# First quads with the mask added by TensorE in PSUM, first products one quad later, summary rows by DMA, and three native groups of w_out

## The chip, the cores and the metric

The kernel runs on one core of a Trainium2 chip. The core has TensorE (matrix products into PSUM), VectorE (shown as DVE), ScalarE (ACT), GpSimd (POOL), SyncE (SP, here the issuer of nearly all transfers) and 16 DMA engines between DRAM and the on-chip memory SBUF. The metric is the device time of one execution in microseconds; the median of several runs is compared. Each engine works through its own instructions in order and waits on semaphores for the others.

## The reference

Inputs: q, k, v of shape (4 batches, 8 heads, 768 positions, 64), and the two weight matrices w_in (512 x 2048) and w_out (2048 x 512), all float32.

```python
k_sum = k.reshape(B, H, nb, block, D).max(axis=3)      # block = 32, nb = 24
v_sum = v.reshape(B, H, nb, block, D).mean(axis=3)
scores_l = scale * np.matmul(q, k.transpose(0, 1, 3, 2))
mask_l = np.abs(pos[:, None] - pos[None, :]) < window  # window = 16
scores_s = scale * np.einsum('bhsd,bhnd->bhsn', q, k_sum) + np.log(block)
scores_all = np.concatenate([np.where(mask_l, scores_l, -1e9), scores_s], axis=-1)
a = softmax(scores_all)
x = matmul(a, concatenate([v, v_sum])) -> (3072 tokens, 512)
h = x @ w_in
sp = np.maximum(h, 0.0) + np.log1p(np.exp(-np.abs(h)))
g = h * erf(sp)
out = g @ w_out
```

So each query sees its neighbours within 15 positions and 24 summaries of the whole sequence; a two-layer network with the activation h · erf(softplus(h)) follows.

## The kernel before, in words

**Tiling.** The 3072 tokens are six chunks of 512. A *quad* is one chunk and one pair of heads: four quads to a chunk, 24 in all. For a quad, the queries are taken in eight blocks of 64; each block needs a window of 96 keys and the 24 summaries, 120 columns. `scores` (line 434 on) makes them on TensorE into two PSUM banks, `softmax` adds the mask (lines 471 and 475), takes the maximum (479), the exponential with a sum (484) and divides (488 to 496). `transp` turns the weights by TensorE (506), ScalarE copies them out (510), and `av` (531) multiplies by the values. `xsplit` splits the result into a high part xh and a low part xl (236 and 547).

A *period* k is one chunk and one of four column groups of the hidden layer: 24 periods. In a period, `mm1` (line 570) makes the four hidden tiles of the group by products in a reduced form of float32: high x high, low x high and high x low, three products for one. `hout`, `logs`, `erfs` (581, 594, 599) compute the activation, `gsplit` multiplies and splits it (606, or 611, 236 and 618), and `mm2` (631 or 635) adds its product with w_out into four banks.

**Two forms of the second product.** For the first chunk `mm2` uses the native float32 product with w_out unsplit (line 631, tile a32s); for all others the split form of three products (line 635). `gsplit` follows: no split of the activation in the first chunk (line 606).

**Weights.** They come in as pairs of 32-bit words and VectorE puts each together in three steps (284, 287, 290). w_in's are split at once by `split`: ScalarE makes the high part (236), VectorE the low part (306). w_out's are put together into slots named in `WHOLE`, and split later by `parts`: groups 2 and 3 in period 3, groups 0 and 1 in period 4. Large SBUF slots w0 to w13 are shared in time. Not all split weights fit, so numbers 4 to 7 are stored to DRAM (`put`) and loaded again for each chunk (`get`) into the slots named in `HOME`.

**The first chunk's quads.** Quads 0 to 3 take their keys straight from the natural layout (tiles kf, qf), their maxima from `ksum_first` (388). The value means come from `vsum_first`: six products with a selection matrix (394), a copy by ScalarE (397), and four copies by GpSimd (399) which spread the 24 mean rows over the eight blocks of each quad's value tile vwf. Their scores lie in the banks pa, h0 and h1, o0 and o1, then h0 and h1 again; the same banks take the first hidden tiles (`hbanks`). After scores and softmax of all four, a loop does transpose, weighted sum, split and the first products of each quad in turn.

**Order.** A planner (class `Plan`) holds all operations with an assumed duration on an engine. `due` sets due times backwards from TensorE's order; `order` then runs a list schedule over the assumed durations, with TensorE allowed to pick among the next operations of its order, and transfers as a serial queue on SP. What comes out is the fixed order of instructions on every engine. Ahead of the first operation on TensorE stand `WARM` fillers (line 673), products of zeros into an unused bank; until the bank o3 is first used, `busy` puts more of them where the plan leaves TensorE idle.

Of the kernel before, what the change touches and what calls it, by code (L numbers as in the profile page):

```python
# [36 lines left out]
WARM = 20  # L37
# [126 lines left out]
def block_attention_mlp(ctx: ExitStack, tc: tile.TileContext, q_t, k_nat, k_win, v_tok, v_nat, v_win, w_in, w_out, out):  # L164
# [67 lines left out]
    def dma(kb, fn, r=(), w=(), **kw):  # L232
        return P.add({"SP": max(0.45, kb / 330.0)}, lambda e: fn(), r, w, **kw)
# [10 lines left out]
    WHOLE = {0: 11, 1: 10, 2: 8, 3: 9}  # L244
    HOME = {0: 12, 1: 13, 2: 11, 3: 8, 4: 9, 5: 10, 6: 9, 7: 10}
# [25 lines left out]
    def convert(u):  # L271

        w, s, m = f"w{raw_slot(u)}", {}, number(u)
        home = f"gl{u[2]}" if u[0] == "i" else f"a{m}"

        def a():
            if u[0] == "i":
# [14 lines left out]
        on({"DVE": 0.69}, lambda e: a(), [w], [home] if u[0] == "i" or u[2] else frees(WHOLE[u[1]]))  # L292
        on({"DVE": 1.22}, lambda e: b(), [w, home], [home])
        on({"DVE": 1.22}, lambda e: c(), [w, home], [home])
        if u[0] == "i":
            split(u, raw_slot(u), home, lambda: s["t"])
# [87 lines left out]
    def load_vw_first(p):  # L384
        dma(393, lambda: nc.sync.dma_start(out=st[p]["vw"][0:LW], in_=v_win[0, p]), w=[f"vwf{p}"])
# [4 lines left out]
    def vsum_first(bank):  # L390
# [7 lines left out]
        for p in range(NP):  # L398
            on({"POOL": 1.3}, lambda e, p=p: e.tensor_copy(st[p]["vw"][LW:NK], vsum[LW:NK, p:p + 1, :].to_broadcast([NS, NB, 128])), [f"vsum0{p}"], [f"vwg{p}"])
# [20 lines left out]
    def load_quad_v(qd):  # L420
# [6 lines left out]
        dma(393, go, w=["vw"])  # L427
# [5 lines left out]
    def scores(qd, banks=("pa",)):  # L433
# [3 lines left out]
        def go():  # L437
# [3 lines left out]
            s["both"] = tiles["pa"] if banks == ("pa",) else None  # L441
            for i in range(NI):
                for c in range(2):
                    j = 2 * i + c
                    for a in range(2):
# [8 lines left out]
                        for n, rhs in parts:  # L454
                            n += i * NK
                            nc.tensor.matmul(sc[a][o, n:n + rhs.shape[-1]], lhsT=s["qb"][r, 64 * j:64 * j + 64], rhs=rhs, start=True, stop=True)  # L456
        if qd >= NP:
            pe(1.06, go, ["qb", "kw"], banks)
        else:
            pe(1.4, go, [f"qf{qd}", f"kf{qd}", f"ksum0{qd}"], banks)  # L460

    def softmax(qd, banks=("pa",)):
# [5 lines left out]
        def add(e):  # L468
            t = s["pr"] = sb([128, 2 * NI, NK], F32, "pr") if qd >= NP else prs[qd // 2][:, qd % 2]
            if s["both"] is not None:  # L470
                e.tensor_tensor(t.rearrange("q (a i) c -> q a i c", a=2), s["both"][:, :, 0:NI * NK].rearrange("q a (i c) -> q a i c", i=NI),  # L471
                                mk.unsqueeze(1).to_broadcast([128, 2, NI, NK]), op=ALU.add)
            else:
                for a in range(2):
                    e.tensor_tensor(t[:, NI * a:NI * a + NI], s["sc"][a][:, 0:NI * NK].rearrange("q (i c) -> q i c", i=NI), mk, op=ALU.add)
# [398 lines left out]
```

## Time and profile before

| | before |
|---|---|
| median of 3 runs, us | 654.64 (654.37 to 656.39) |
| the profiled execution's own time, us | 654.22 |
| its span, first to last instruction, us | 652.4 |
| mean granted TensorE clock | 0.997 |
| instructions | 10447 |
| TensorE products busy | 642.3 us, 98% |
| VectorE busy | 399.6 us, 61% |
| ScalarE busy | 429.5 us, 66% |
| GpSimd busy | 24.1 us, 4% |
| moved by DMA | 89.02 MB, mean 136 GB/s |

The profile is one execution recorded by the hardware. A line of a group names the line of the kernel, the engine, the operation, the tile written and the tile read, shapes and count; after the bar stand the busy time in all, the mean of one in nanoseconds, and the idle time of that engine just before, with what ended it. A float32 product is recorded as two records in the native form. The chain of waits is followed backwards from the last instruction, at each step to what released it. "issue" is time in which an engine waited for nothing that the profile shows.

### The profile page before, as it was taken

What the parts mean: (1) busy time and instruction counts of PE and PEld (TensorE: products, weight loads), DVE (VectorE), ACT (ScalarE), POOL (GpSimd) and SP (SyncE); (2) the same over time, 40 slices, a digit from 0 to 9 for tenths busy, and PEclk for the clock granted to TensorE, in tenths of its full rate; (3) what the DMA queues carried; (4) which work ended last, traced back from release to release, by engine and by line L of the source; (5) the groups of instructions that cost most, each with busy time, mean ns of one, the idle gap of its engine ahead of it and who ended that gap; (6) DMA issues with size and microseconds to landing.
All of it is one profiled execution on the core that took longest, in us unless ns stands there. A gap on an engine that the chain in (4) does not pass through costs nothing.

```text
span 652.4 us, 10447 instructions
## 1 busy us (share of the span) xinstructions
PE 642.3 (98%) x4216; PEld 497.7 (76%) x4224; DVE 399.6 (61%) x507; ACT 429.5 (66%) x770; POOL 24.1 (4%) x52
## 2 busy tenths in 40 slices
PE   9799999999999999999999999999999999999997
PEld 4477656657588888888888888888888888888886
DVE  4899999866666755656656556456457355334432
ACT  2476999787976675865854964945866754763570
POOL 3301000000000000000000000000000000000000
PEclk9899999999999999999999999999999999999999
DMA  8997654355373425464315442206352103140014
GB/s 323 286 333 264 225 142 158 130 205 206 108 272 90 126 62 168 159 227 109 102 37 194 132 151 66 78 1 206 85 186 77 31 0 115 65 144 1 1 51 143
DMA packets 27872, 89.02 MB, mean 136 GB/s; under 512 B 2992, under 2 KB 7856, under 8 KB 22704
## 3 DMA queue, kind: packets, MB, share of 16 engines
q1 hardware_dynamic: 27248, 87.83, 41.9%
q8 instruction: 33, 0.54, 0.3%
q10 hardware_dynamic: 576, 0.52, 0.2%
q14 instruction: 15, 0.12, 0.1%
HBM read 75.89 MB, written 10.49 MB: 132 GB/s over the span
## 4 chain that ended last, share of the span: by engine, by line
PE 97%; ACT 1%; issue 1%; DVE 0%
PE h L570 39%; PE ops L635 34%; PE ops L631 9%; PE px L531 4%; PE idle L673 3%; PE pa L456 3%; PE pa L506 3%; PE vs L394 1%; PE h L456 0%; ACT L832 0%; PE vt L352 0%; PE o L456 0%; ACT wt L581 0%; ACT wt L594 0%; ACT ptr L510 0%
## 5 line engine op out<-in xcount | busy, mean ns | idle before, releaser
L570 PE MATMUL h<-xh,w 128*128 128x512 f32 x768 | 250.9, 397 | 0.0
L635 PE MATMUL ops<-w,gh 128*128 128x512 f32 x640 | 202.1, 392 | 0.0
L570 PEld LDWEIGHTS h<-xh,w 128*128 128x128 f32 x768 | 144.2, 188 | 32.6 <-issue 1.5
L581 ACT ACTIVATE wt<-h 128x512 f32<-128x512 f32 x96 | 56.8, 596 | 144.9 <-DVE hc L236 79.3
L570 PE MATMUL h<-xl,w 128*128 128x512 f32 x384 | 149.6, 389 | 0.0
L635 PEld LDWEIGHTS ops<-w,gh 128*128 128x128 f32 x640 | 120.5, 188 | 25.2
L236 DVE COPY hc<-h 128x512 f32<-128x512 f32 x90 | 62.0, 690 | 125.8 <-PE h L570 117.6
L832 ACT ACT_TABLE_LOAD x105 | 134.7, 1283 | 1.8
L635 PE MATMUL ops<-w,gl 128*128 128x512 f32 x320 | 124.6, 389 | 0.0
L570 PEld LDWEIGHTS h<-xl,w 128*128 128x128 f32 x384 | 72.2, 188 | 16.4 <-issue 1.9
L635 PEld LDWEIGHTS ops<-w,gl 128*128 128x128 f32 x320 | 60.1, 188 | 12.0
L484 ACT ACTIVATE pr<-pr,stats 128x120 f32<-128x120 f32 x160 | 60.9, 382 | 9.7 <-DVE stats L492 9.6
L611 DVE TENSOR_TENSOR hc<-wt,hc 128x1024 f32<-128x1024 f32 x40 | 47.7, 1223 | 18.6 <-ACT wt L599 18.6
L631 PE MATMUL ops<-a32s,gw 128*128 128x512 f32 x128 | 58.1, 596 | 0.0
L594 ACT ACTIVATE wt<-wt,stats 128x1024 f32<-128x1024 f32 x48 | 55.3, 1152 | 0.6
L599 ACT ACTIVATE wt<-wt 128x1024 f32<-128x1024 f32 x48 | 49.2, 1054 | 0.3
L618 DVE TENSOR_TENSOR gl<-hc,gh 128x1024 fp32r<-128x1024 f32 x40 | 47.5, 1219 | 0.2
L236 DVE CAST gh<-hc 128x1024 fp32r<-128x1024 f32 x40 | 27.3, 690 | 24.6 <-PE ops L635 24.0
L631 PEld LDWEIGHTS ops<-a32s,gw 128*128 128x128 f32 x128 | 23.4, 190 | 24.5 <-issue 23.9
L484 ACT ACTIVATION_READ_ACCUMULATOR pr<-pr,stats 128x1 f32 x160 | 29.9, 187 | 0.0
L417 POOL COPY kw<-ksum 128x96 f32<-128x96 f32 (+1 forms) x28 | 12.7, 465 | 455.2 <-DMA kw<-k_win 373.4
L471 DVE TENSOR_TENSOR pr<-pa,mask_sb 128x960 f32<-128x960 f32 x20 | 23.1, 1155 | 10.3 <-PE pa L456 10.3
(84 smaller groups left out, 511.0 us busy)
## 6 DMA issues: line engine op xcount, KB each, us to landing
w<-dr SPq DMA_DIRECT2D x20, 1024.0 KB, 4.8
kw<-k_win SPq DMA_DIRECT2D x20, 480.0 KB
rw<-w_in SPq DMA_DIRECT2D x8, 1024.0 KB, 5.1
rw<-w_out SPq DMA_DIRECT2D x8, 1024.0 KB, 4.8
vw<-v_win SPq DMA_DIRECT2D x20, 384.0 KB, 4.9
qb<-q_t SPq DMA_DIRECT2D x20, 256.0 KB, 5.5
out<-ob SPq DMA_DIRECT2D x20, 256.0 KB, 4.9
kvn<-v_nat SPq DMA_DIRECT2D x12, 384.0 KB, 4.6
```

The lines of the kernel that those rows point to most:

```text
L236: e.copy(o, i) if e is nc.scalar else e.tensor_copy(o, i)
L484: nc.scalar.activation(s["pr"][:, j], s["pr"][:, j], AF.Exp, scale=0.125, bias=s["mx"][:, j:j + 1], accum_out=sm[:, j:j + 1])
L531: nc.tensor.matmul(xo[r, o], lhsT=s["vw"][:, j, r], rhs=s["pt"][:, a, o], start=True, stop=True)
L570: nc.tensor.matmul(hs[k, f][:, 0:T], lhsT=w[m], rhs=xt[ch, cc][x], start=(cc == 0 and n == 0), stop=(cc == 3 and n == 2))
L581: nc.scalar.activation(wt[k, f // 2][:, f % 2], hs[k, f][:, 0:T], AF.Tanh, scale=0.5)
L594: act(1.15, lambda n=n: nc.scalar.activation(wt[k, n], wt[k, n], AF.Ln, scale=-0.49999994, bias=half_b), [s], [s], table="log")
L599: act(1.05, lambda n=n: nc.scalar.activation(wt[k, n], wt[k, n], AF.Erf, scale=-1.0), [s], [s], table="sig", after=after)
L611: e.tensor_tensor(hc[k, n], wt.pop((k, n)), hc[k, n], op=ALU.mult)
L618: e.tensor_tensor(gs[k, n][1], hc.pop((k, n)), f32(gs[k, n][0]), op=ALU.subtract)
L631: nc.tensor.matmul(os_[ch, t], lhsT=x[0][:, i % 2, t * 128:(t + 1) * 128], rhs=w32["o", g, i // 2][:, i % 2], start=first, stop=last)
L635: nc.tensor.matmul(os_[ch, t], lhsT=x[y][:, i % 2, t * 128:(t + 1) * 128], rhs=w[m], start=first and n == 0, stop=last and n == 2)
L832: nc.scalar.preload_act_table_set(sets[o["load"]])
```

## The change

- **Mask.** For the first four quads, `scores` first puts the mask into each bank by a float32 product of the unit matrix and the mask table, 480 columns, two a quad; the scores are added onto it. `softmax` has no add for these quads: the maximum is taken from PSUM in two halves, and the exponentials read PSUM and write the weights to SBUF. They therefore also hold the banks.
- **First products.** In the loop over the first quads, the first products of quad p - 1 stand after the weighted sum of quad p; those of quad 3 after the loop.
- **Summary rows.** The spreading of the mean rows stays on GpSimd for quad 0 and is a DMA on SP for quads 1 to 3.
- **Native groups.** The native form is used while k < `NN` = 3. Period 3's activation is split, and w_out's group 3 is split as soon as it is put together, in place in slots 12 and 13, from where `mm2` of period 3 reads it. `WHOLE` loses its fourth entry, `HOME` is new, `parts` of numbers 4, 5 and 0 run in period 3 through slot 9 and those of 1 to 3 in period 5; the first `get` of group 2 is in period 5 in place of 4.
- **Fillers and the planner's prices.** `WARM` goes from 20 to 11; the planner is told 310 instead of 330 KB to a microsecond for transfers, 520 instead of 393 KB for the value windows, and 3.0 instead of 1.4 us for the first quads' scores.

```diff
-WARM = 20
+WARM = 11
+NN = 3
...
-        return P.add({"SP": max(0.45, kb / 330.0)}, lambda e: fn(), r, w, **kw)
+        return P.add({"SP": max(0.45, kb / 310.0)}, lambda e: fn(), r, w, **kw)
...
-    WHOLE = {0: 11, 1: 10, 2: 8, 3: 9}
-    HOME = {0: 12, 1: 13, 2: 11, 3: 8, 4: 9, 5: 10, 6: 9, 7: 10}
+    WHOLE = {0: 11, 1: 10, 2: 8}
+    HOME = {0: 9, 1: 12, 2: 11, 3: 13, 4: 10, 5: 8, 6: 10, 7: 8}
...
     def convert(u):
-        home = f"gl{u[2]}" if u[0] == "i" else f"a{m}"
+        at_once = u[0] == "i" or u[1] >= NN
+        home = f"gl{u[2]}" if at_once else f"a{m}"
...
-        if u[0] == "i":
+        if at_once:
             split(u, raw_slot(u), home, lambda: s["t"])
...
     def load_vw_first(p):
-        dma(393, ...
+        dma(520, ...
...
         for p in range(NP):
-            on({"POOL": 1.3}, lambda e, p=p: e.tensor_copy(st[p]["vw"][LW:NK], vsum[LW:NK, p:p + 1, :].to_broadcast([NS, NB, 128])), [f"vsum0{p}"], [f"vwg{p}"])
+            if p == 0:
+                on({"POOL": 1.1}, lambda e: e.tensor_copy(st[0]["vw"][LW:NK], vsum[LW:NK, 0:1, :].to_broadcast([NS, NB, 128])), ["vsum00"], ["vwg0"])
+            else:
+                dma(100, lambda p=p: nc.sync.dma_start(out=st[p]["vw"][LW:NK], in_=vsum[LW:NK, p:p + 1, :].to_broadcast([NS, NB, 128])), [f"vsum0{p}"], [f"vwg{p}"])
...
     def scores(qd, banks=("pa",)):
+            if qd < NP:
+                for a in range(2):
+                    nc.tensor.matmul(sc[a][:, 0:NI * NK], lhsT=ident, rhs=mask_sb[:, 0:NI].rearrange("q i c -> q (i c)"), start=True, stop=False, skip_group_check=True)
...
-                            nc.tensor.matmul(sc[a][o, n:n + rhs.shape[-1]], lhsT=s["qb"][r, 64 * j:64 * j + 64], rhs=rhs, start=True, stop=True)
+                            nc.tensor.matmul(sc[a][o, n:n + rhs.shape[-1]], lhsT=s["qb"][r, 64 * j:64 * j + 64], rhs=rhs, start=qd >= NP, stop=True, skip_group_check=True)
...
-            pe(1.4, go, [f"qf{qd}", f"kf{qd}", f"ksum0{qd}"], banks)
+            pe(3.0, go, [f"qf{qd}", f"kf{qd}", f"ksum0{qd}"], banks)
...
     def softmax(qd, banks=("pa",)):
         def red(e):
             s["mx"] = stat(0, par)
-            e.tensor_reduce(s["mx"], s["pr"], op=ALU.max, axis=AX.X)
+            if qd >= NP:
+                e.tensor_reduce(s["mx"], s["pr"], op=ALU.max, axis=AX.X)
+                return
+            s["pr"] = prs[qd // 2][:, qd % 2]
+            for a in range(2):
+                e.tensor_reduce(s["mx"][:, NI * a:NI * a + NI], s["sc"][a][:, 0:NI * NK].rearrange("q (i c) -> q i c", i=NI), op=ALU.max, axis=AX.X)
...
-                nc.scalar.activation(s["pr"][:, j], s["pr"][:, j], AF.Exp, scale=0.125, bias=s["mx"][:, j:j + 1], accum_out=sm[:, j:j + 1])
+                i = j % NI
+                nc.scalar.activation(s["pr"][:, j], s["pr"][:, j] if qd >= NP else s["sc"][j // NI][:, i * NK:(i + 1) * NK], AF.Exp, scale=0.125, bias=s["mx"][:, j:j + 1], accum_out=sm[:, j:j + 1])
...
-        on({"DVE": 1.15}, add, banks, [pr])
-        on({"DVE": 1.12}, red, [pr], [f"mx{par}"])
+        if qd >= NP:
+            on({"DVE": 1.15}, add, banks, [pr])
+        on({"DVE": 1.12 if qd >= NP else 1.2}, red, [pr] if qd >= NP else banks, [f"mx{par}"])
...
-        s["exps"] = act(3.25, exps, [f"mx{par}"], [pr, f"sm{par}"], table="log")
+        s["exps"] = act(3.25, exps, [f"mx{par}"] + ([] if qd >= NP else list(banks)), [pr, f"sm{par}"], table="log")
...
     def gsplit(k, n, mult, cast, sub):
-        if k < NG:
+        if k < NN:
...
     def mm2(k, fs=range(G), ts=range(NT)):
-            if ch == 0:
+            if k < NN:
...
-                    pe(0.685, lambda i=i, t=t: go(i, t), [f"w{HOME[m]}", f"gh{i // 2}", f"gl{i // 2}"], [f"o{t}"])
+                    pe(0.685, lambda i=i, t=t: go(i, t), [f"w{HOME[m] if ch else 12 + m % 2}", f"gh{i // 2}", f"gl{i // 2}"], [f"o{t}"])
...
         transp(p)
         av(p, "o2")
         xsplit(p, {"DVE": 0.69, "ACT": 0.6})
-        for f in range(G):
-            mm1(0, f, (p,))
+        if p:
+            for f in range(G):
+                mm1(0, f, (p - 1,))
+    for f in range(G):
+        mm1(0, f, (NP - 1,))
...
         if k == 3:
-            for m in range(4, 8):
-                parts(m, 12 + m % 2)
+            for m in (6, 7):
                 put(m, 12 + m % 2)
-        if k == 4:
-            for m in range(4):
+            for m in (4, 5):
+                parts(m, 9)
+                put(m, 9)
+            parts(0, 9)
+        if k == 5:
+            for m in (1, 2, 3):
                 parts(m, HOME[m])
...
-        if k >= NG and g in (0, 3):
+        if k == NG + 1 or k > NG + 1 and g in (0, 3):
             for r in range(2):
-                get(6 + r if g else 4 + r)
+                get(6 + r if g == 3 else 4 + r)
```

More of the change, by code (lines that the diff above doesn't have):

```diff
@@ L290, in c @@
             nc.vector.scalar_tensor_tensor(s["a"], s["rw"][..., 1], 0xC0000000, s["a"], op0=ALU.bitwise_and, op1=ALU.bitwise_or)
-        on({"DVE": 0.69}, lambda e: a(), [w], [home] if u[0] == "i" or u[2] else frees(WHOLE[u[1]]))
+        on({"DVE": 0.69}, lambda e: a(), [w], [home] if at_once or u[2] else frees(WHOLE[u[1]]))
         on({"DVE": 1.22}, lambda e: b(), [w, home], [home])
         on({"DVE": 1.22}, lambda e: c(), [w, home], [home])
-        if u[0] == "i":
+        if at_once:
             split(u, raw_slot(u), home, lambda: s["t"])
@@ L384, in load_vw_first @@
     def load_vw_first(p):
-        dma(393, lambda: nc.sync.dma_start(out=st[p]["vw"][0:LW], in_=v_win[0, p]), w=[f"vwf{p}"])
+        dma(520, lambda: nc.sync.dma_start(out=st[p]["vw"][0:LW], in_=v_win[0, p]), w=[f"vwf{p}"])
     def ksum_first(p):
@@ L426, in go @@
             nc.sync.dma_start(out=s["vw"][0:LW], in_=v_win[ch, p])
-        dma(393, go, w=["vw"])
+        dma(520, go, w=["vw"])
         for b, js in seqs:
@@ L468, in add @@
         def add(e):
[L469 to L475, printed above, removed]
+            t = s["pr"] = sb([128, 2 * NI, NK], F32, "pr")
+            e.tensor_tensor(t.rearrange("q (a i) c -> q a i c", a=2), s["both"][:, :, 0:NI * NK].rearrange("q a (i c) -> q a i c", i=NI),
+                            mk.unsqueeze(1).to_broadcast([128, 2, NI, NK]), op=ALU.add)
         def red(e):
             s["mx"] = stat(0, par)
-            e.tensor_reduce(s["mx"], s["pr"], op=ALU.max, axis=AX.X)
+            if qd >= NP:
[4 more added lines that the diff above has]
+                e.tensor_reduce(s["mx"][:, NI * a:NI * a + NI], s["sc"][a][:, 0:NI * NK].rearrange("q (i c) -> q i c", i=NI), op=ALU.max, axis=AX.X)
         def exps():
@@ L638, in mm2 @@
                 m = 2 * g + i // 2
-                if ch == 0:
+                if k < NN:
                     pe(0.87, lambda i=i, t=t: go(i, t), [f"a{m}", f"gh{i // 2}"], [f"o{t}"])
                 else:
-                    pe(0.685, lambda i=i, t=t: go(i, t), [f"w{HOME[m]}", f"gh{i // 2}", f"gl{i // 2}"], [f"o{t}"])
+                    pe(0.685, lambda i=i, t=t: go(i, t), [f"w{HOME[m] if ch else 12 + m % 2}", f"gh{i // 2}", f"gl{i // 2}"], [f"o{t}"])
     def evac(ch, t):
```

## The prediction

> **What bounds the kernel now.** I read the page's busy times first, then the chain of waits in order of time, then busy times by stretch. The page's line for the engines:
>
> ```profile
> PE 642.3 (98%) x4216; PEld 497.7 (76%) x4224; DVE 399.6 (61%) x507; ACT 429.5 (66%) x770; POOL 24.1 (4%) x52
> ```
>
> TensorE sets the end. But its 98% hides fillers: matmuls of line 673 that compute nothing. The chain's first 75 us (start, length, what):
>
> ```profile
> by line: PE idle L673 30.0%; PE h L570 26.1%; PE vs L394 7.4%; issue 6.7%; PE px L531 6.1%; PE ops L631 6.0%; PE pa L506 5.9%; PE h L456 4.1%; PE pa L456 3.4%; PE o L456 2.4%; DVE zeros L218 0.4%; PE vt L352 0.3%; DVE vs_sum L201 0.2%; DVE
> 1.34 6.44 PE idle L673 x20
> 7.78 1.54 PE pa L456 x37
> 9.33 2.77 PE vs L394 x6
> ...
> 23.24 0.90 PE px L531 x25
> 24.14 3.97 issue
> ...
> 28.72 5.30 PE idle L673 x16
> 34.02 0.87 PE pa L506 x8
> 34.89 2.75 PE h L570 x12
> ...
> 38.31 1.08 PE px L531 x32
> ...
> 39.55 1.24 PE idle L673 x5
> ...
> 52.23 2.32 PE idle L673 x10
> 54.55 2.90 PE h L570 x12
> ...
> 64.39 2.54 PE idle L673 x11
> ...
> 66.95 4.53 PE ops L631 x10
> ```
>
> 30.0% of 75 us are 22.5 us of fillers, and 6.7% are 5.0 us of gaps, nearly all before 66.95. From there TensorE runs full. By stretch (length, busy time per engine):
>
> ```profile
> 34.00:51.90 17.90, 17.69 (x172) 13.60 (x172) 16.28 (x23) 10.60 (x33) 0.26 (x1) 1.00 0.97 331
> 51.90:67.00 15.10, 14.97 (x93) 9.92 (x94) 14.90 (x20) 12.06 (x20) 2.12 (x3) 1.00 0.78 275
> ...
> 130.00:182.00 52.00, 52.00 (x310) 32.78 (x303) 34.39 (x43) 42.62 (x87) 1.94 (x3) 1.00 0.53 178
> ```
>
> So a gain comes in two ways only: less TensorE work after 66.95 (there it counts in full), or an earlier start of the full stretch. Before it, VectorE (third number, 16.28 of 17.90 and 14.90 of 15.10) and the transfers (share 0.97, 0.78) are tight.
>
> **Part 1: three native groups in place of four.** The second products of period 3 leave the native form (line 631) for the split form (line 635). Rows of the chain:
>
> ```profile
> 107.96 9.64 PE ops L631 x22
> 215.59 10.91 PE ops L635 x48
> ```
>
> A native call is two records: 9.64/22 × 2 = 0.876 us. A split call is three: 10.91/48 × 3 = 0.682. There are 16 calls in a group: 16 × 0.194 = **3.1 us less** TensorE work, after 66.95, in full. For it VectorE gets two casts and two subtractions, by the page 690 and 1219 ns:
>
> ```profile
> L618 DVE TENSOR_TENSOR gl<-hc,gh 128x1024 fp32r<-128x1024 f32 x40 | 47.5, 1219 | 0.2
> L236 DVE CAST gh<-hc 128x1024 fp32r<-128x1024 f32 x40 | 27.3, 690 | 24.6 <-PE ops L635 24.0
> ```
>
> That is 2 × (0.69 + 1.22) = 3.8 us in period 4, which lies in the stretch from 130 to 182, where VectorE is idle 17.6 of 52 us: nothing on the path, 3.8 at most if that cover is gone. The splits of w_out are eight as before, only placed elsewhere (two at once, three in period 3, three in period 5). The reloads of split weights stay 20; those of groups 4 and 5 first run in period 5 instead of 4, queued on SP past that period's other loads, and are needed in period 7. The four stores to DRAM remain; two now go through slot 9 in turn. I cost these at nothing.
>
> **Part 2: the mask by TensorE.** Each first quad gets two fp32 products of 128x128 by 480 columns. No row has that shape; the native call gives 0.876 × 480/512 = 0.82 us, the summary product of line 394 (chain row at 9.33: 2.77 for three calls) gives 0.92 × 480/512 = 0.87. I take 0.82: 1.64 a quad, **6.6 us** in all (6.9 at most).
>
> The first 1.64 stands where nine fillers went. The mask table is written by 5.73:
>
> ```profile
> 5.62 0.11 POOL L198 MEMSET mask_sb<- 64x16 f32 x1
> ```
>
> so masks run to about 7.5, scores (1.54) to 9.1, against 9.32 before: no loss, and no filler fewer would help, because of the table. Quads 1 to 3 bring 4.9. Between 9.4 and 23.24 TensorE has 2.4 us of fillers besides its work:
>
> ```profile
> L673 PE MATMUL idle<-zeros 128*128 128x512 bf16 x8 | 2.4, 379 | 0.3 <-issue 0.2
> ```
>
> so the first weighted sum slips by 4.9 − 2.4 = 2.5, from 23.24 to about 25.7; the slip ends in the 3.97 us gap and the 5.30 us of fillers after it.
>
> VectorE loses the adds and reduces from PSUM in halves instead:
>
> ```profile
> L479 DVE TENSOR_REDUCE stats<-prf 128x8 f32<-128x960 f32 x4 | 4.6, 1144 | 0.0
> L475 DVE TENSOR_TENSOR prf<-h,mask_sb 128x480 f32<-128x480 f32 x4 | 2.4, 648 | 0.6 <-PE h L456 0.6
> L471 DVE TENSOR_TENSOR prf<-pa,mask_sb 128x960 f32<-128x960 f32 x1 | 1.2, 1158 | 4.5 <-PE pa L456 4.5
> ```
>
> Gone are 1.16 + 6 × 0.65 = 5.1 us; a half reduction from PSUM I bound by 0.57 (half of 1144) and 0.65 (the half add from PSUM): 0 to +0.6. Net about −4.6. The exponentials read PSUM instead of SBUF: count unchanged, costed at nothing. But they now hold the banks: the quads in h0, h1 and o0, o1 free them only when ScalarE is done, and there the first products go.
>
> **Part 3: summary rows by DMA.** Three of the four GpSimd copies go. While they ran, VectorE was slowed:
>
> ```profile
> 20.53 5.98 POOL L399 COPY vwf<-vsum 24x1024 f32<-24x1024 f32 x4 [13.99 <-ACT vsum L397]
> ```
>
> ```profile
> 23.63 1.98 DVE L290 SCALAR_TENSOR_TENSOR a<-rw,a 128x1024 uint32<-128x1024 uint32 x1
> ...
> 30.16 1.22 DVE L306 TENSOR_TENSOR w<-a,w 128x1024 fp32r<-128x1024 f32 x1 [2.39 <-ACT w L236]
> ...
> L290 DVE SCALAR_TENSOR_TENSOR a32s<-rw,a32s 128x1024 uint32<-128x1024 uint32 x8 | 9.8, 1222 | 0.0
> ```
>
> The first of these takes 1.98 where its kind in w_out's conversions takes 1.22: 0.8 us lost, and none where a single copy runs elsewhere. VectorE's relief before 30 us is thus up to 4.6 + 0.8 = 5.4, and up to 7.8 if its 2.39 us idle wait goes as well; it can also be nothing, where VectorE then merely waits for data.
>
> The price is time to arrive. In this stretch the SP queue is backed up: the one load of the first value windows whose landing the trace resolves took 15.2 us from issue.
>
> ```profile
> L385 SPq DMA_DIRECT2D vwf<-v_win x4: 328/328/342, 9.1 to 18.4; - x4
> DMA to landing us min/median/max: 15.2/15.2/15.2
> ```
>
> The sums are copied out when the GpSimd copies start, 20.5, now some 2.5 later: 23.0; rows of quad 1 then land at about 38.2. Their issues wait on SP for the copied sums, and behind them there wait quad 4's loads (keys, queries, values) and then w_out; these lose nothing, as the queue is full anyhow. The planner's raised prices for transfers change no instruction, only the order it writes; I cost that at nothing, within rival (a). For a lower bound, 5 us as the page's median for an unhurried load (4.9 for vw<-v_win), rows at 27.9.
>
> ```profile
> vw<-v_win SPq DMA_DIRECT2D x20, 384.0 KB, 4.9
> ```
>
> [...]
>
> **Part 4: first products a quad later.** Before, the order is transpose, weighted sum, then the products of the same quad, which wait for its high and low parts: the fillers at 39.55 and 52.23 are such waits. Now quad p's products fill the wait of quad p+1. From the second weighted sum on, TensorE has: that sum 1.08, transpose 0.87, products 2.77, sum 1.08, transpose 0.87, products 2.75, sum 1.08, the split of its result into high and low parts, two steps of about 0.68 (the row below is one of them), then the last products 2.90: 14.8 us.
>
> ```profile
> L547 DVE TENSOR_TENSOR xl<-px,xh 128x512 fp32r<-128x512 f32 x24 | 16.4, 682 | 1.4 <-ACT xh L236 1.4
> ```
>
> If the sum starts at 38.2, about where it starts now (38.31), the first products end at 53.0, against 54.55 + 2.90 = 57.45: **4.5 us earlier**. VectorE, tight in this stretch, has 5.4 us less to do, so it allows that. I carry 4.5 on to 66.95, since VectorE is as tight between the two points before and after. Ends: nothing gained, and 7.8; if the rows were there by 27.9, VectorE's 7.8 would be the limit.
>
> **The sum.** 654.22 (the profiled execution's own time; span 652.4) − 3.1 − 4.5 = 646.6. The median of the runs, 654.64, is 0.4 above that execution: **647**.
>
> **Rivals.** (a) *Late rows, slower.* The rows are placed on SP behind quad 4's loads, the last issued at 28.01.
>
> ```profile
> 28.01 0.33 SPq L426 DMA_DIRECT2D vw<-v_win  x1
> ```
>
> Each issue holds the queue and each landing took 15.2, so the three come at 43 to 48. Each microsecond past 38.2 is lost one for one; past 38.2 + 4.5 + 3.1 = 45.8 the kernel is slower. At 48: 647 + 9.8 = 656.8 as a median. For it: share 0.97 of the transfers. Against: rows are needed before quad 4's loads, and the order on SP goes by due times.
>
> (b) *Banks held.* If the last quad's exponentials still run until 39.65 as now (row below: the last reading starts at 39.45), products that wrote h0 at 34.89 wait 4.8 us; a loss in place of the gain: 654.2 − 3.1 + 4.8 = 655.9, within 2 us of the median: no measurable change. For it:
>
> ```profile
> 39.45 0.20 ACT L484 ACTIVATION_READ_ACCUMULATOR prf<-prf,stats 128x1 f32 x1
> ```
>
> [...]
>
> (c) *Nothing at the front.* VectorE's relief falls into its own waits: 651.1 to 651.5, the native group alone.
>
> (d) *The gap goes.* The 3.97 us gap waits for no semaphore. In it, one transfer of a queue of 33, 16 KB each, arrives:
>
> ```profile
> q8 instruction: 1, 0.02, 2.0%
> ```
>
> PE and PEld have 8,440 records, 256 for each of the 33: TensorE's program arriving late behind data. Records before it in the new order are nearly as many (−18 for fillers, +32 for masks), so I keep the gap. If it falls away, up to 4.0 us more: 642.6, or 643 as a median. [...]
>
> **How the numbers follow.** Below 0.3% (2 us) this kernel's runs cannot be told from no change. Forecast (645 to 650.5) 0.46; (d) 0.11; (c) 0.13; these are faster, 0.70. (b) and half-late rows, between 652.7 and 656.6: 0.13. (a) 0.17. The range runs from 642 to 656, leaving out some of (a) and a front with both (d) and VectorE's whole 7.8. Most of the chance is on one side.
>
> **What would show it.** Right: line 635's products at 960 + 48 = 1008 records and line 631's at 96; the start of the full stretch near 62.4; no fillers over 1 us between the weighted sums; one POOL copy; VectorE's last conversion step near 1.22 in the first 30 us too. Wrong at part 3: TensorE waits before the second weighted sum for a DMA from vsum past 40 us. Wrong at part 2: products wait for exponentials. Wrong at part 1: VectorE over 90% from 130 to 182 with TensorE idle there. The whole fails if TensorE's full stretch begins after 70 us.

## The result, and the profile after

The changed kernel takes 645.61 us (median of 4 runs, 645.06 to 645.99); the kernel before, beside it, 655.51 (654.37 to 656.57). The ratio is 0.9849, with a 95% interval from 0.9826 to 0.9871: 1.5% faster. The profiled execution took 645.62 us, 8.6 less than the profiled one of before (654.22). Of 53 executions of the kernel before that ran beside the experiments, the 12 with a mean granted TensorE clock of 0.999 or more took 649.9 to 652.1 us and the other 41, at 0.994 to 0.997, 652.5 to 656.6, so some 4 us of the gain stand only against those 41.

The engines on the page of the changed kernel (busy time, share of the span, instructions):

```profile
span 643.8 us, 10416 instructions
PE 636.3 (99%) x4210; PEld 498.7 (77%) x4210; DVE 399.6 (62%) x509; ACT 433.8 (67%) x773; POOL 18.6 (3%) x49
```

TensorE's busy time falls by 6.0 us only, since fillers and work count alike in it. The chain of waits in order of time (start, length, what) shows the front:

```profile
16.30 5.34 PE vs L396 x12
21.64 1.61 PE h L450 x4
23.25 1.54 PE h L465 x37
24.80 1.02 PE pa L518 x8
...
27.02 1.15 PE px L543 x32
28.18 1.02 PE pa L518 x8
29.19 1.51 PE idle L685 x7
30.70 1.39 PE h L582 x6
32.09 1.08 PE px L543 x32
```

Line 450 is the mask product, 465 the scores, 396 the value sums, 518 the transposes, 543 the weighted sums, 582 the first products, 685 the fillers. The first weighted sum (27.02) now runs through without a gap; before, it stood still for 3.97 us. The second comes at 32.09 (before 38.31). Before, TensorE's granted clock also fell to 0.50 after the gap, for 3.41 us from 29.22 on; in the changed kernel it stays at 1.00. A row by stretch of the kernel before has this as a mean of 0.87 (third number from the end):

```profile
30.00:40.00 10.00, 9.84 (x71) 6.02 (x71) 9.45 (x14) 7.56 (x35) 0.26 (x1) 0.87 1.04 292
```

Two rows of TensorE's work in order of time, the last of the first chunk's first products in period 0 and the first second-product, give the ends of the front:

```profile
48.48 0.39 PE L582 MATMUL h<-xh,w 128*128 128x512 f32 x1
...
58.44 0.67 PE L643 MATMUL ops<-a32s,gw 128*128 128x512 f32 x1
```

The first products end near 48.7 in place of 57.45, and the stretch in which TensorE is full starts at 58.44 in place of 66.95: **8.5 us earlier**. Further on, one and the same weighted sum stands in the chain before at

```profile
214.26 1.08 PE px L531 x32
```

and in the chain of the changed kernel at

```profile
205.57 1.08 PE px L543 x32
```

which is 8.7 us earlier, and so it stays to the end. Between 58 and 205 us the native group gives TensorE 3.1 us less to do, yet only 0.2 us more is won there: some 2.9 us were lost. In sight are 2.06 of them, two waits of TensorE that the kernel before did not have (in brackets the idle time before the instruction); the other 0.8 were not found:

```profile
87.73 0.50 PE L582 MATMUL h<-xh,w 128*128 128x512 f32 x1 [0.91 <-ACT wt L593]
...
173.88 0.95 PE L465 MATMUL pa<-kw,qb 64*64 64x120 f32 x28 [1.15 <-issue]
```

Busy times by stretch of the changed kernel (TensorE, its weight loads, VectorE, ScalarE, GpSimd) say who was full then; columns as in the prediction:

```profile
30.00:46.85 16.85, 16.85 (x163) 12.85 (x161) 16.53 (x20) 7.88 (x11) 1.33 (x2) 1.00 0.98 289
46.85:90.00 43.15, 42.15 (x242) 27.47 (x242) 40.26 (x51) 42.73 (x72) 1.50 (x5) 1.00 0.77 268
```

Up to 46.85 it is VectorE (16.53 of 16.85). After it, ScalarE is busy 42.73 of 43.15 us. The chain that ended last runs through ScalarE nearly without a break from 46.87 to 87.7. Of that time, table loads are the largest part, 14 of them (groups of ScalarE in that stretch):

```profile
L850 ACT ACT_TABLE_LOAD x14 | 18.0, 1283 | 0.2
```

### The profile page after: what moved, and what is told of

Its sections match the earlier page's. It is cut to its first block, busy times and chain, and to the rows that moved or that the text cites. A ratio compares the mean times of both kernels' runs of the same rounds, so it can differ in the third digit from the quotient of the medians.

```text
span 643.8 us, 10416 instructions
## 1 busy us (share of the span) xinstructions
PE 636.3 (99%) x4210; PEld 498.7 (77%) x4210; DVE 399.6 (62%) x509; ACT 433.8 (67%) x773; POOL 18.6 (3%) x49
## 4 chain that ended last, share of the span: by engine, by line
PE 92%; ACT 7%; issue 0%; DVE 0%; ACTq 0%
PE h L582 37%; PE ops L647 36%; PE ops L643 4%; PE px L543 4%; PE pa L518 3%; PE pa L465 3%; ACT L850 3%; PE idle L685 1%; ACT wt L593 1%; ACT pr L495 1%; PE vs L396 1%; ACT wt L606 1%; ACT wt L611 1%; PE h L450 1%; PE h L465 0%
## 5 line engine op out<-in xcount | busy, mean ns | idle before, releaser
L647 PE MATMUL ops<-w,gh 128*128 128x512 f32 x672 | 212.6, 392 | 0.0
L647 PEld LDWEIGHTS ops<-w,gh 128*128 128x128 f32 x672 | 126.5, 188 | 26.5 <-issue 0.2
L647 PE MATMUL ops<-w,gl 128*128 128x512 f32 x336 | 130.9, 389 | 0.0
L647 PEld LDWEIGHTS ops<-w,gl 128*128 128x128 f32 x336 | 63.1, 188 | 12.6
L623 DVE TENSOR_TENSOR hc<-wt,hc 128x1024 f32<-128x1024 f32 x42 | 50.2, 1223 | 19.1 <-ACT wt L611 19.1
L630 DVE TENSOR_TENSOR gl<-hc,gh 128x1024 fp32r<-128x1024 f32 x42 | 50.1, 1220 | 0.3
L237 DVE CAST gh<-hc 128x1024 fp32r<-128x1024 f32 x42 | 28.8, 691 | 24.7 <-PE ops L647 24.0
L643 PE MATMUL ops<-a32s,gw 128*128 128x512 f32 x96 | 43.5, 596 | 0.1
L643 PEld LDWEIGHTS ops<-a32s,gw 128*128 128x128 f32 x96 | 17.5, 190 | 18.6 <-issue 17.7
L499 DVE TENSOR_SCALAR stats<-stats 128x8 f32<-128x8 f32 x24 | 4.9, 203 | 37.9 <-ACT pr L495 37.9
```

The lines of the kernel that those rows point to most:

```text
L237: e.copy(o, i) if e is nc.scalar else e.tensor_copy(o, i)
L623: e.tensor_tensor(hc[k, n], wt.pop((k, n)), hc[k, n], op=ALU.mult)
L630: e.tensor_tensor(gs[k, n][1], hc.pop((k, n)), f32(gs[k, n][0]), op=ALU.subtract)
L643: nc.tensor.matmul(os_[ch, t], lhsT=x[0][:, i % 2, t * 128:(t + 1) * 128], rhs=w32["o", g, i // 2][:, i % 2], start=first, stop=last)
L647: nc.tensor.matmul(os_[ch, t], lhsT=x[y][:, i % 2, t * 128:(t + 1) * 128], rhs=w[m], start=first and n == 0, stop=last and n == 2)
```

## The experiments

Three questions were left: what each part of the change is worth, alone and in company; what took the gap in the first weighted sum away, SP's wait for the sums with the weights behind it (the "held queue" below) or TensorE's new order; and which engine took 2.9 us back. The kernel before, run beside them, went from 649.9 to 656.6 us from one execution to another (medians 654.5 to 655.1), the changed kernel from 645.06 to 645.99. So the intervals of the ratios are some 0.3% to either side, and the variants of the changed kernel are also compared by their own medians and ranges. Each profile is one execution, and times of two profiles can differ by 0.6 us from the start: the first eleven fillers take 4.88 us in the changed kernel's and 4.30 in that of experiment 2.

**1. The native group alone.** The kernel before with `NN = 3` and all that belongs to it:

```diff
+NN = 3
...
-            if ch == 0:
+            if k < NN:
```

with the new `WHOLE` and `HOME`, `convert`, `gsplit`, `parts`, `put` and `get` of the change.

> The kernel before with one part of the change: three native groups of w_out in place of four, with its slots, splits and reloads; the first quads are as before. By the first theory (the native group's 16 calls go from 0.876 to 0.682 us each, in full on TensorE's path) 3.1 us less: 654.6 to 655.5 becomes 651.5 to 652.4. By the rival (VectorE's added 3.8 us and the later splits make TensorE wait) no gain, 654.5 or more.

Measured: 652.04 us (before 655.06; ratio 0.9943, 0.9916 to 0.9969), 3.0 us less. The first theory holds: alone, the part is worth what the sum gave it. At like clocks the difference is the same: its four executions with a granted clock of 1.00 took 647.4 to 648.9 us, those of the kernel before with 0.999 or more 650.8 to 651.5.

**2. The front alone.** The changed kernel with the native form for four groups:

```diff
-            if k < NN:
+            if ch == 0:
```

and the old `WHOLE`, `HOME`, splits and reloads.

> The changed kernel with four native groups again, as before; everything at the front stays changed. If the two parts add up, the front is worth what is left, 9.5 - 3.1: some 6.4 us less than before, 648.7. If the front's gain was partly eaten by waits that the third period's splits cause (TensorE lost some 2.9 us between its first second-product and 205 us), then more than that: 647 or less.

Measured: 646.63 us (646.30 to 647.26; ratio 0.9881, 0.9848 to 0.9914). The front is worth 8.4 us (some 4.4 against those 650.8 to 651.5), and beside it the native group is worth only 1.0 (646.63 to 645.61, ranges apart). The number of the second reading holds: the parts don't add up, 3.0 + 8.4 against 9.4 to 9.9 in all (645.61 against the 655.06 here and the 655.51 beside it). Its reason, the splits, isn't what the trace shows. In this kernel's TensorE waits only the first of the two named above is left:

```profile
PE h L581 <- ACT wt L592: 0.9, 1, 0.9
```

The 1.15 us at 173.88 comes with the native group's change: there TensorE's order has the scores right behind the transposes of another quad, in the same bank, which ScalarE first has to copy out (it copies from 172.77 to 173.78).

**3. Rows from ScalarE's queue.**

```diff
-                dma(100, lambda p=p: nc.sync.dma_start(out=st[p]["vw"][LW:NK], ...
+                act(0.5, lambda p=p: nc.scalar.dma_start(out=st[p]["vw"][LW:NK], ...
```

> The changed kernel with the three row transfers issued from ScalarE's queue in place of SP's, so that SP no longer waits 10.9 us for the copied sums with the weights queued behind. By the theory that this wait emptied the transfer queue and so let TensorE's program arrive in time (its block came at 21.1 us, against 25.5 before), the gap of some 4 us comes back inside or near the first weighted sum, at about the 700th TensorE record, and the full stretch starts 2 to 4 us later than 58.4; the time 646 to 649. By the rival (the gap went because of the new order on TensorE itself) no gap, weights earlier, and 645.6 or less.

Measured: 653.50 us (651.19 to 654.10; ratio 0.9991, 0.9966 to 1.0016): all of the gain is gone. But the gap is not the one expected. The chain of this kernel (the profiled execution is its shortest, 651.19 at a granted clock of 0.997; the other nine had 0.991 to 0.994):

```profile
26.52 1.08 PE px L543 x32
...
29.48 0.95 PE h L582 x3
30.43 4.62 issue
35.05 1.95 PE px L543 x32
```

The first weighted sum (26.52) runs through; the 700th TensorE record is passed there without a stop, and the block of the program that it needs had started at 20.24 us though SP held nothing back. The stop is before the *second* weighted sum, till 35.05, and that sum takes 1.95 us in place of 1.08, as the granted clock is 0.50 for 3.41 us from 35.11 on. ScalarE is stuck as well: the third row transfer is issued at 34.98, and ScalarE does nothing from 30.0 to then (rows of its queue and of ScalarE in order of time):

```profile
21.69 2.25 ACTq L404 DMA_DIRECT2D vwf<-vsum  x2
24.04 1.05 ACT L237 CAST w<-a 128x1024 fp32r<-128x1024 f32 x1 [2.38 <-DMA vwf<-vsum]
...
34.98 0.82 ACTq L404 DMA_DIRECT2D vwf<-vsum  x1
```

So the theory of the held queue, as the reason why the gap went, has fallen. What this run does show is the harm that the prediction's rival (a) spoke of: with the loads running on ahead, the second weighted sum waits, to 35 in place of 32.09, and ScalarE, whose queue holds the third row transfer, waits with it. What the two waited for, the rows or the windows loaded into the same tile, the trace doesn't say, so that late rows are the cause is not shown.

**4. Rows by GpSimd again.** All four copies on GpSimd, as before.

```diff
-            if p == 0:
-                on({"POOL": 1.1}, ...
-            else:
-                dma(100, ...
+            on({"POOL": 1.3}, lambda e, p=p: e.tensor_copy(st[p]["vw"][LW:NK], ...
```

> The changed kernel with all four row copies on GpSimd, as before. By the theory of the held queue the gap comes back (SP holds no more) and VectorE is slowed again while GpSimd copies, 0.8 us or more: the full stretch starts 3 to 6 us later than 58.4, the time 648 to 651. By the rival (who copies the rows does not matter once the mask is on TensorE) 645.6 within 1 us.

Measured: 646.53 us (645.56 to 647.58; ratio 0.9879, 0.9840 to 0.9917), 0.9 more than the changed kernel, with ranges that overlap. Its four executions are two pairs: 645.56 and 645.76 at a granted clock of 0.999 or more, as the changed kernel, and 647.29 and 647.58 at 0.996 and 0.997. No gap came back at the front, and the block was in time (20.4 us). The rival holds: who copies the rows hardly matters, and this too goes against the held queue. VectorE's loss to the copies is there, as in the kernel before, on another instruction (chain of this kernel: 1.89 where 1.22 is usual):

```profile
25.44 1.89 DVE w L308
```

**5. Products with their own quad again.**

```diff
-        if p:
-            for f in range(G):
-                mm1(0, f, (p - 1,))
-    for f in range(G):
-        mm1(0, f, (NP - 1,))
+        for f in range(G):
+            mm1(0, f, (p,))
```

> The changed kernel with each first quad's products right after its own weighted sum again, as before. By the prediction's part 4 (products a quad later fill the wait for the split) the waits between the weighted sums come back, some 4 us of fillers, and the first products end near 51 in place of 46.9; since ScalarE is full from there on, 3 to 5 us of it reach the end: 649 to 650. By the rival (the planner may pick among the next operations anyhow) nothing changes: 645.6 within 1 us.

Measured: 647.39 us (647.24 to 647.70; ratio 0.9915, 0.9876 to 0.9954): 1.8 more. (The 46.9 in the expectation was misread, it is where the chain leaves TensorE; the products end at 48.7.) The direction is the theory's, the size at the end about half of it: TensorE's full stretch starts at 62.01 in place of 58.44, 3.6 us later, but half of that is made up behind it. The fillers between the weighted sums are back, but they are 0.81 and 1.67 us:

```profile
32.88 1.08 PE px L543 x32
...
35.04 0.81 PE idle L685 x3
35.85 2.76 PE h L582 x12
38.61 1.08 PE px L543 x32
...
40.76 1.67 PE idle L685 x7
42.44 2.75 PE h L582 x12
```

**6. The mask by VectorE again.** Adds, reduction and exponentials of the first quads as before, no mask products; the rest of the change stays.

```diff
-                for a in range(2):
-                    nc.tensor.matmul(sc[a][:, 0:NI * NK], lhsT=ident, rhs=mask_sb[:, 0:NI]...
...
-        if qd >= NP:
-            on({"DVE": 1.15}, add, banks, [pr])
+        on({"DVE": 1.15}, add, banks, [pr])
```

> The changed kernel with the mask added by VectorE again in the first quads: no mask products, adds and reductions as before, the exponentials in SBUF. By the prediction's part 2 (mask products stand where fillers were, and VectorE is relieved of 4.6 us) the full stretch starts up to 4.6 us later: 647 to 650. By the rival (6.6 us of mask products lie on TensorE's path at the front and cost as much as VectorE's adds) 645.6 within 1 us, or faster.

Measured: 649.94 us (649.22 to 651.55; ratio 0.9945, 0.9922 to 0.9968): 4.3 more, the largest single part. The theory's range holds, but its reason isn't the whole: a gap stands in this kernel's chain, in the scores of the third quad,

```profile
14.24 1.14 PE o L461 x30
15.38 2.29 issue
17.66 0.46 PE o L461 x5
```

and a 16 KB block of the program started to come in at 15.10 us, just ahead of it. Counted in the trace (TensorE's products, weight loads and a few semaphore instructions), this gap stands after 448 records. In the native group's kernel (1.) there are two such, at 17.34 and 25.57 us, after 447 and 702 records, in two different kinds of work; its chain:

```profile
16.07 1.26 PE o L458 x29
17.34 1.21 issue
...
24.67 0.90 PE px L533 x25
25.57 3.97 issue
```

Among the transfers of that kernel there is one of the queue of 16 KB blocks in the stretch from 15.9 to 17.3 us (it started at 15.93), and one in the stretch from 25.5 to 29.6 (it started at 27.03); between 18.6 and 25.5 there is none (queue, count, MB, share of the 16 engines; one answer for each stretch):

```profile
q8 instruction: 1, 0.02, 5.2%
```

```profile
q8 instruction: 1, 0.02, 1.8%
```

702 is also where it stood in the kernel before, and 702 − 447 = 255 is a block of 256 (8,440 records to 33 transfers) but for one instruction. What is more, in all five stops of this kind (one in the kernel before, the one above, the two just named, and one in 10.) TensorE goes on 1.3 to 1.5 us after the transfer has ended: 26.72 and 28.11 before, 17.09 and 18.55, 28.23 and 29.54 in the native group's kernel, 16.18 and 17.66 above, 15.86 and 17.36 in 10. This settles what the gap is: TensorE at the end of a block of its program, with the next one late.

The 4.3 us are not all the mask's. The full stretch of this kernel starts at 60.87, 2.4 us after 58.44, and the late block lies ahead of that. The rest arises behind it: a wait of 1.99 us for VectorE at 89.16, where the changed kernel waits 0.91 for ScalarE, and then a granted clock of 0.50 for 3.41 us from 91.85 on, by estimate 1.7 us of TensorE's work (0.5 × 3.41); the changed kernel's later wait of 1.15 us does not occur. All ten executions had a granted clock of 0.995 or 0.997.

**7. Moving the block boundary.** The kernel before with 24 small fillers more:

```diff
     busy(WARM)
+    for _ in range(24):
+        nc.tensor.matmul(idle[:, 0:32], lhsT=zeros[:, 0:128], rhs=zeros[:, 0:32], start=True, stop=True)
```

> The kernel before with 24 fillers of 32 columns more right after the first 20, 48 TensorE records in all and about 2 us. The gap of 3.97 us before the 702nd TensorE record, inside the first weighted sum: if it is TensorE's program arriving late in blocks of 256, it stays before about the 702nd record and so moves 48 records forward in the work, to the last quad's scores. If it is a wait of the weighted sum, it stays inside the weighted sum, at about the 750th record.

Measured, one execution: 650.89 us, with hardly a gap left: the block started at 20.99 us, 4.2 after TensorE had entered the block before it (8.7 in the kernel before), and was in at 22.25. The stop that is left lasts 0.15 us. It stands where the first theory puts it, after 702 records, which is now after the first product of the weighted sum and not after the 25th, so 24 products or 48 records further forward in the work (TensorE's rows):

```profile
23.77 1.15 PE L531 MATMUL px<-ptr,vwf 120*64 120x64 f32 x31 [0.15 <-issue]
25.07 3.62 PE L673 MATMUL idle<-zeros 128*128 128x512 bf16 x16 [0.16 <-issue]
```

TensorE again goes on 1.5 us after the transfer's end. So the test bears out what the counts under 6 say, and it shows that the same transfer order can bring the block early or late. It also prices the gap. The 16 fillers after the sum take 3.62 us here and 5.30 in the kernel before, where the granted clock was 0.50 for most of that time. Behind them TensorE waits 1.95 us here, for VectorE, so not all of the gap comes back: the second weighted sum starts at 35.12 in place of 38.31 and the full stretch at 63.71 in place of 66.95, 3.2 us earlier, with some 0.6 us of fillers more. The time is near the low end of the spread of the kernel before.

**8. Logarithms cut short.** Periods 0 to 2 take the logarithm over 64 of 512 columns, so most of that step is left out there; order and plan are the same.

```diff
-nc.scalar.activation(wt[k, n], wt[k, n], AF.Ln, ...
+nc.scalar.activation(*(2 * [wt[k, n] if k > 2 else wt[k, n][:, :, 0:64]]), AF.Ln, ...
```

> The changed kernel with the logarithm of periods 0 to 2 taken over 64 columns in place of 512, which leaves out most of that step there; the order of all instructions is the same. It takes some 0.9 us from each of six ScalarE instructions, 5 us in all. By the theory that ScalarE is the bound from 47 to 87 us, where it is busy 42.7 of 43.2 us, TensorE's waits at 87.7 and later go: 2 to 3 us less, 643 to 644. By the rival (VectorE, 40.3 of 43.2, or the split of period 3 costs those 2.9 us) no change: 645.6 within 0.7 us.

Measured: 644.11 us (643.93 to 644.43; ratio 0.9855, 0.9824 to 0.9886): 1.5 less than the changed kernel, ranges apart. ScalarE held the kernel for about that much; TensorE's wait at 87.7 shrinks from 0.9 to 0.2, the one of 1.1 near 172 stays, as the cut logarithms end before it:

```profile
PE pa L465 <- issue: 1.1, 1, 1.1
PE h L582 <- ACT wt L593: 0.2, 1, 0.2
```

**9. Fewer table loads.** The planner shuns a change of ScalarE's table by 2.5 us in place of 1.5; no operation is left out.

```diff
-... + (1.5 if ops[n]["table"] not in (None, table) and e == "ACT" else 0.0), n))
+... + (2.5 if ops[n]["table"] not in (None, table) and e == "ACT" else 0.0), n))
```

> The changed kernel with the planner told to shun a change of ScalarE's table by 2.5 us in place of 1.5; its program then holds 105 table loads in place of 109, two of the four in the first 100 us. By the theory that ScalarE is the bound between 47 and 87 us (there it spends 18.0 of 43.2 us on 14 table loads of 1.28) up to 2.6 us less there and TensorE's waits shrink: 643 to 644.5. By the rival (ScalarE's fullness costs nothing, the waits come from the bank order) 645.6 within 0.7 us.

Measured: **643.23 us** (643.04 to 644.20; ratio 0.9834, 0.9806 to 0.9862): 2.4 less than the changed kernel, ranges apart, and the fastest kernel here that leaves nothing out. In the stretch below it has 12 table loads in place of 14. Stretch and waits of this kernel:

```profile
46.85:90.00 43.15, 43.10 (x246) 28.31 (x246) 40.45 (x50) 41.74 (x73) 3.95 (x5) 1.00 0.82 288
PE pa L465 <- issue: 0.4, 1, 0.4
```

ScalarE gets air (41.74 of 43.15), TensorE is busy 43.10 in place of 42.15, and of its 2.06 us of waits 0.4 are left. With 8., this shows that ScalarE took 1.5 us or more of the 2.9 back. How much of the 2.4 is the table loads alone is not shown, as the order changed with them.

**10. Rows by DMA alone.** The kernel before with only the rows of quads 1 to 3 on SP.

```diff
-            on({"POOL": 1.3}, ... for all p
+            if p == 0: on({"POOL": 1.1}, ...
+            else: dma(100, ...
```

> The kernel before with one part of the change: rows of quads 1 to 3 by DMA on SP. If the late blocks of TensorE's program come from the traffic of the weights, SP's wait for the sums empties the queue here as well, the block is in before the 702nd TensorE record, and the time is 650 to 651. If they come from how fast TensorE runs through its records before, the gap stays at record 702, and the time is 654 to 656, with VectorE's 0.8 us at most to the good.

Measured: 652.51 us (650.30 to 654.27; ratio 0.9966, 0.9943 to 0.9988), between the two. Its profile (an execution of 654.27, its longest) has no gap after record 702 but one after 448:

```profile
14.76 0.99 PE o L459 x27
15.76 1.60 issue
17.36 0.48 PE o L459 x9
```

Neither theory is borne out: the late block has moved one boundary ahead. And in this profile the held queue has a price. SP waits 11.1 us for the sums; a load of w_in, issued behind, is in at 54.6, and from there the chain of waits runs through VectorE; TensorE waits 1.26 us at 55.32 and 0.85 at 64.33, and its full stretch starts at 65.19, where 7., without the rows, has 63.71.

**11. Twenty fillers at the start.**

```diff
-WARM = 11
+WARM = 20
```

> The changed kernel with 20 fillers at the start as before. By the prediction (the mask products stand where nine fillers went) the front slips by the nine fillers, about 2 us, and what ScalarE lets through reaches the end: 646.5 to 647.5. By the rival (the first quads wait for keys, not for TensorE) 645.6 within 0.5 us.

Measured: 646.88 us (646.35 to 647.24; ratio 0.9888, 0.9856 to 0.9919): 1.3 more, as the first theory expected. The first 20 fillers take 6.57 us in place of 4.88 for eleven, and the full stretch starts at 59.80 in place of 58.44.

**12. Old prices for transfers.**

```diff
-        return P.add({"SP": max(0.45, kb / 310.0)}, ...
+        return P.add({"SP": max(0.45, kb / 330.0)}, ...
```

and 393 in place of 520 for the value windows.

> The changed kernel with the planner's old prices for transfers (330 KB a microsecond, 393 for the value windows): instructions are the same, only their order differs. By the prediction, which costed these at nothing, 645.6 within 1 us. By the rival (the order on SP that lets rows and weights come in time rests on the new prices) rows or weights late by some us: 648 or more.

Measured: 645.31 us (645.12 to 645.88; ratio 0.9866, 0.9835 to 0.9897): no difference. The prices did nothing here.

## Why the prediction was right, and where it was not

The time forecast, 647, is 1.4 above the measured 645.6, and the sign was right, as was the view that TensorE's full stretch sets the end. That the number came so close is in part luck: the front brought 4.0 us more than its term of the sum, and 2.9 were lost behind it at a place where the sum has nothing. Point by point:

**Part 1, "3.1 us less TensorE work, in full".** Alone it measured 3.0, so the price of a call was right. "In full" failed: beside the new front it was worth 1.0. The step that failed is the one that looked for cover on VectorE only, in the stretch from 130 to 182 us; VectorE did have room (35.85 of 52 us busy there in the changed kernel). TensorE's wait there, 1.15 us at 173, comes from the new order, which puts two uses of a bank next to each other with a copy by ScalarE between. The remaining 1 us was not found; the wait behind ScalarE at 87 stands with four native groups too (2.).

**Part 2, the mask.** Four masks cost 1.84, 1.81, 1.81 and 1.61 us in the chain, 7.1 in all, a little above the 6.9 given as the most. That they replace fillers was right (11.: the nine fillers are worth 1.3). The first weighted sum came at 27.02, expected at about 25.7. VectorE's half reductions from PSUM take 0.65, the upper bound:

```profile
L489 DVE TENSOR_REDUCE stats<-h 128x4 f32<-128x480 f32 x4 | 2.4, 653 | 3.3 <-PE h L465 3.3
```

Undoing this part costs 4.3 us. At the start of the full stretch it is 2.4, and a late block of 2.29 us lies ahead of that; the rest arises behind, where the clock is halved for a while (6.).

**Part 3, rows by DMA.** "Rows at 38.2" was too late: the second weighted sum starts at 32.09. SP did wait for the sums, with the weights queued behind it, 10.9 us; I had costed that wait at nothing for the loads and had not seen that the queue runs dry behind it (the transfers' share from 22 to 24 us is 0.42); the rows, issued from 22.29 on, were in within 9.8 us in place of 15.2 (waits of SP in the first 60 us of the changed kernel):

```profile
SPq L404 <- ACT vsum L399: 10.9, 1, 10.9
```

The part as a whole is worth 0.9 us at most to tell (4.), and nothing is left of it between the executions at a granted clock of 0.999 or more. With GpSimd's copies the second weighted sum starts at 31.98, so the rows are hardly what it waits for at 32.09 in the changed kernel.

**Part 4, products a quad later.** Right in direction, 1.8 us. With the other order the same quads' waits measured 0.81 and 1.67. The sum of 14.8 us from the second weighted sum to the end of the products has an error: it holds the products of three quads, and by the change those of quad 0 stand behind that sum as well. Measured, from 32.09 to 48.7, it is 16.6 us.

**The front, "4.5 us earlier".** It was 8.5. In the prediction's own terms, the second weighted sum came 6.1 us ahead of its 38.2 (32.09), and what follows took 1.8 longer than its 14.8: the term that was mis-sized is the arrival of the rows. The 3.97 us gap, which I kept, rival (d), has its part in this. Without it the kernel before has its second weighted sum at 35.12 (7.), 3.2 us ahead of 38.31; the change brings the other 3.0. But a gap that is over at 28.11 could not hold a sum that waits for rows until 38.2, so the "up to 4.0 us more" of (d) did not fit the sum beside it, and 8.5 − 4.5 = 4.0 is near the gap's length by chance.

The step on the gap that failed is "records before it in the new order are nearly as many, so I keep the gap". The number of records may be right, but what counted here is the time between two boundaries. Before, TensorE entered one block at 16.73 us and stood at its end at 24.14, 7.4 us later, and the next block landed 10.0 us after the entry. In the changed kernel the same stretch of records takes 11.7 us (15.90 to 27.63), since a pair of masks (1.61 us in eight records) and all the value sums fall into it (5.34 us; 1.91 of them before); even a block 10.0 us late would have been in time. It came after 6.3. Why a block takes 5 to 6 us in one kernel and 10 or 11 in another is open: it isn't SP's held queue (3., 4.), and the shift (7.) changed it without a change in the transfers' order.

**The rivals.** (a) did not occur; a second weighted sum held up to 35 did in experiment 3, with late rows as one possible cause. (b) did not occur, if only just: the last quad's exponentials end at 30.1, and the first products start at 30.35, when the split of the first weighted sum, which they need, is done. (c) did not occur. (d) did; in the kernel before it is worth 3.2 us (7.), not 4.0.

**The signs.** Line 635's products came to 1008 records and line 631's to 96, POOL has one copy, and VectorE's last conversion step takes 1.22 us in the first 30 us too. The full stretch starts at 58.44 and not near 62.4, and "no fillers over 1 us between the weighted sums" failed: 1.51 us of them stand between the first and the second.

**The carry, "VectorE is as tight between the two points before and after".** This held: 8.7 us at the end of the first products are still 8.5 at 58.44. What failed is the step behind it, "From there TensorE runs full", by which nothing is lost from there on. Behind that point ScalarE is full. The prediction quoted its busy time (12.06 of 15.10 from 51.9 to 67) and did not ask what it becomes once TensorE starts 8.5 us earlier: 14.95 of 15.10. Of the 2.9 us lost, 0.91 are a wait behind ScalarE, 1.15 the wait at the bank, and 0.8 were not found; experiments 8 and 9, which took time off ScalarE, brought 1.5 and 2.4 us.

## What to carry to other kernels

Once a front is shortened, look again for the engine that is full right behind it: two gains that measure 3.0 and 8.4 us apart came to 9.5 together, and an order with four table loads fewer then brought 2.4 more. Before a gain is booked, compare the granted clock of the executions on both sides: some 4 us here stand only against executions at 0.994 to 0.997. A gap that no semaphore explained, at the same count of records in different work (447 or 448, and 702), was TensorE's program arriving late here; ask then how many microseconds the engine takes for a block of its program (7.4 before, with the gap, and 11.7 after, without); to put long instructions where transfers are dense is a remedy that was not tested by itself. A transfer that waited held what was queued behind it: SP's loads for 10.9 us, ScalarE's work from 30.0 to 34.98 in experiment 3; whether three of them stood in SP's or in ScalarE's queue made 8 us here.

## What the runs showed of the hardware

- **Late program blocks.** While transfers kept the 16 DMA engines full (their share was 1.00 at the stop of the kernel before, 1.15 and 0.99 at the two stops of 1., 1.03 at the one of 6., 0.96 from 5 to 35 us in 10.), TensorE stopped after 447 or 448 and after 702 records for 1.2 to 4.0 us, each time with a 16 KB transfer of its program that started within the stop or up to 1.4 us ahead of it (native group alone: 15.93 ahead of the stop at 17.34, 27.03 in the stop from 25.57; mask by VectorE: 15.10 ahead of 15.38; rows by DMA alone: 14.79 ahead of 15.76). It went on 1.3 to 1.5 us after the transfer's end. The times of the kernel before (649.9 to 656.6) follow the granted clock of the execution, as said with the result; the profile with the stop has 0.997, the one of 7., with next to none, 1.00. That the stop makes the spread is likely, not shown: each kernel was profiled once.
- **Half the clock after a stop.** The granted clock of TensorE fell to 0.50 for 3.41 us in the kernel before (from 29.22, after the stop of 3.97 us from 24.14), in 3. (from 35.11, after 4.62 from 30.43) and in 6. (from 91.85, after 1.99 from 89.16), and for 6.83 us in 1. (from 28.06, in the stop from 25.57). While it lasted, 16 fillers took 5.30 us in place of 3.62, and a weighted sum 1.95 in place of 1.08. Not every stop brought it: that of 1.95 us in 7. and the one of 2.29 in 6. did not. What decides is open.
- **Exponentials read from PSUM are closer together.** The eight of a quad start 0.38 us apart when they read SBUF (13.49, 13.89, 14.27 and on in the kernel before), and 0.34 when they read PSUM, the first pair 0.35 (the changed kernel, 11.17, 11.52, 11.86 and on):

```profile
11.17 0.36 ACT L495 ACTIVATE prf<-pa,stats 128x120 f32<-128x120 f32 x1 [9.14 <-DVE stats L504]
11.43 0.19 ACT L495 ACTIVATION_READ_ACCUMULATOR prf<-pa,stats 128x1 f32 x1
11.52 0.35 ACT L495 ACTIVATE prf<-pa,stats 128x120 f32<-128x120 f32 x1
```

- **The same row transfers in two queues.** Behind SP's wait of 10.9 us, the sum that needs the first of them started 9.8 us after the first issue (22.29 to 32.09). Issued from ScalarE's queue, with SP's loads running on, it started 13.4 us after (21.69 to 35.05). When the rows landed is resolved in neither trace, so that the fuller queue slowed the rows themselves is not shown.
